# Local attention as banded matmuls in chunks that run into the next layer's prologue, and one softmax check at the end in place of flags and branches

## The chip, the cores and the metric

The kernel runs on one core of one Trainium2 chip. The metric is device time in microseconds (us). The engines are PE (TensorE), DVE (VectorE), ACT (ScalarE), POOL (GpSimd) and SP (SyncE, which here issues DMAs).

## The reference

Four layers work on 2048 tokens of width 512, each with a layer norm and a residual. Layers 1 and 3 ("A") are local attention: 32 heads of 16, and each token looks at itself and the seven tokens at distances 2, 4, ... 14 before it. Layers 2 and 4 ("B") are full attention with 32 query heads and one shared key/value head. Shortened:

```python
def _A_ref(x, wqkv, wo):                       # H = 32, Dh = 16, W, dil = 8, 2
    q, k, v = ...                              # (x @ wqkv) split in heads
    idx = pos[:, None] - (jnp.arange(W) * dil)[None, :]
    logits = einsum("bhsd,bhswd->bhsw", q, k[idx]) * Dh ** -0.5   # -1e9 where idx < 0
    o = einsum("bhsw,bhswd->bhsd", softmax(logits), v[idx])
    return merge(o) @ wo
def _B_ref(x, wq, wk, wv, wo):                 # one k and v of width 16 for all heads
    p = softmax(einsum("bhqd,bkd->bhqk", q, k) * Dh ** -0.5)
    return merge(einsum("bhqk,bkd->bhqd", p, v)) @ wo
x = A_x
x = x + _A_ref(layernorm(x), A_wqkv, A_wo);  x = x + _B_ref(layernorm(x), B_wq, B_wk, B_wv, B_wo)
# ... and both once more, with the same weights
```

## The kernel before

Layer A puts 4 chunks of 512 tokens on 4 partition groups and computes each of the 8 window positions as elementwise products on DVE, which PE sums over the head dimension through an identity matrix. Its steps follow each other over the whole sequence.

```python
def layer_A_ch(...):
    ...
    last = layernorm_T(...)                    # all 16 token tiles: norm, transpose
    for d in range(DH):
        proj(0, d)                             # q: 16 matmuls of 512 columns and one ACT copy
        proj(1, d)                             # k
    if NCH > 1:
        nc.sync.dma_start(out=K[32:PCH, :, 0:PAD], in_=K[0:PCH - 32, :, 512:KW])
    for w in range(W):
        lg = ps1.tile([PCH, 512], F32, name="lg", tag="ps1")
        for hf in range(2):
            nc.vector.tensor_tensor(out=prod[:], in0=Q[:, dsl, :],
                                    in1=K[:, dsl, PAD - DIL * w:PAD - DIL * w + 512], op=ALU.mult)
            for d in range(DP):
                nc.tensor.matmul(lg[:], lhsT=ident[:PCH, :PCH], rhs=prod[:, d, :], ...)
        ...                                    # scale, mask the first tokens, running maximum
    ...                                        # v projection, subtract, exp, sum, reciprocal, multiply
    ...                                        # attn * v on DVE, summed on PE; output projection; residual
    if fill_end:
        pe_filler(nc, scratch[:], ident[:], wo_r4[:, 0, :], fill_end)
```

Layer B has a prologue (norm, q/k/v, and a bound on the norms of q and k) which writes a flag. The flag is loaded to a register and picks a fast or a slow attention, so there is a branch around each B:

```python
def layer_B(...):
    prologue_B(tc, x_sb, wq_sb, ..., flag_slot, ...)
    ...
    if mode == "fast":
        fast()
    ...
    else:                                      # mode "auto", as the kernel runs
        cond = nc.values_load(flag_slot, min_val=0, max_val=1)
        with tc.If(cond > 0) as cmp:
            fast()
        with cmp.Else():
            slow()
```

The end of the fast B is a serial chain: copy the last output block out of PSUM, send the softmax sums through DRAM to spread them over partitions, multiply (on POOL), project, add.

```python
def normalize(b, X, S2):
    chain("dve", nc.vector.reciprocal(out=S2[:], in_=S2[:]))
    ...                                        # DMA S2 -> rd (DRAM), DMA rd -> lb (broadcast)
    nc.gpsimd.tensor_tensor(out=onc[qc][:, t, :], in0=X[:], in1=lb[:], op=ALU.mult)
...
for qi in range(4):                            # after the last step
    emit_y(NQC - 1, qi, (opp, dvp)[qi % 2], ("o_ps", "dv")[qi % 2])   # 4 matmuls with woB, then the add
    run_later(10 ** 9)
```

## Time and profile before

The median is 1880.2 us (three runs, 1879.33 to 1886.67; a fourth, counted in the result below, makes it 1880.72); the profiled execution took 1883.3 us. The first view below is of the kernel before, cut into its four stages: A plus B's prologue, B's attention, and both again. The columns are the stretch, its length, then busy time and instruction count of each engine, granted clock, DMA share and GB/s.

```profile
core 0: us, PE busy (x) PEld busy (x) DVE busy (x) ACT busy (x) POOL busy (x), PEclk, DMA share, GB/s
0.00:227.00 227.00, 171.61 (x1598) 96.45 (x1610) 156.88 (x240) 80.05 (x121) 18.96 (x48) 0.97 0.12 32
227.00:945.00 718.00, 591.90 (x5683) 190.38 (x5688) 682.78 (x1116) 690.72 (x512) 23.36 (x16) 0.98 0.05 11
945.00:1162.00 217.00, 173.14 (x1599) 98.78 (x1610) 145.01 (x213) 75.64 (x116) 14.97 (x24) 0.91 0.01 2
1162.00:1880.00 718.00, 569.90 (x5682) 196.46 (x5688) 675.58 (x1088) 689.70 (x512) 23.50 (x16) 0.98 0.06 14
```

B is full: ACT is busy 690 of 718 us. The two A stages, 227 and 217 us, are not: PE is busy 76 and 80%, DVE 69 and 67%. The change is aimed at those.

The second view is the timeline of the kernel before where the first B ends and the third layer starts (columns: start, busy time, engine and line, operation, output from inputs, shape, count, and in brackets the idle time before and what ended it):

```profile
914.60 8.37 ACT L522 ACTIVATE pt<-st 128x1536 bf16<-128x1536 f32 x6
...
932.80 3.60 SPq L587 DMA_DIRECT2D lb<-rd  x8
938.18 1.26 POOL L591 TENSOR_TENSOR onc<-X,lb 128x512 bf16<-128x512 f32 x1 [37.37 <-DMA lb<-rd]
939.50 0.61 PE L598 MATMUL o_ps<-woB_sb,onc 128*128 128x512 bf16 x1 [12.92 <-POOL onc L591]
...
945.21 0.69 DVE L609 TENSOR_TENSOR x_sb<-x_sb,dv 128x512 f32<-128x512 f32 x1 [0.23 <-PE dv L598]
...
949.78 0.38 DVE L91 TENSOR_SCALAR ln_ve<-mv_next 128x4 f32<-128x4 f32 x4 [2.94 <-issue]
951.48 0.81 ACT L99 ACTIVATE xn<-x_sb,ln_nmr,ln_rstd 128x512 bf16<-128x512 f32 x1 [28.51 <-DVE ln_nmr L93]
953.94 4.91 PE L109 MATMUL pT<-ident,xn 128*128 128x128 bf16 x36 [8.77 <-DVE xn L103]
```

The last attention exponential (`pt`) ends at 914.60 + 8.37 = 922.97. The DMA chain for the last sums ends at 938 (PE waits 12.9 us for it), the last residual add at 945.9, and only then does the next layer start; its first transposes (`pT`) run at 953.94, 31.0 us after the last exponential. I use these marks for all kernels: first and last `pt` of each B, first transposes, first projection. The stretch from B1's last exponential to B2's first is called the gap; here it is 239.2 us.

### The profile page before, as it was taken

How to read it: one execution, taken by the hardware profiler on the slowest of the kernel's cores; microseconds unless marked ns; L12 is line 12 of the kernel's file. 1: busy time of each engine (PE TensorE's matmuls, PEld its weight loads, DVE VectorE, ACT ScalarE, POOL GpSimd, SP SyncE). 2: the span in 40 equal slices, each digit the busy share in tenths (PEclk: the TensorE clock that was granted, in tenths of full speed). 3: DMA queues.
4: the chain of work that ended last, by engine and by line, in shares of the span. 5: the costliest groups of instructions: out<-in, count | busy, mean ns of one | idle time of the engine just before them, and what ended most of it. 6: DMA issues, size and time to landing. Idle time of an engine off the chain costs nothing.

```text
span 1883.3 us, 35972 instructions
## 1 busy us (share of the span) xinstructions
PE 1506.5 (80%) x14548; PEld 582.1 (31%) x14596; DVE 1660.3 (88%) x2657; ACT 1536.1 (82%) x1261; POOL 80.8 (4%) x104
## 2 busy tenths in 40 slices
PE   5888787878888887898677887777788788877884
PEld 4443322222222222222163443222222222222221
DVE  4797599999999999999628976999999999999995
ACT  5231599999999999999652326999999999999994
POOL 2001000000000000000010010000000000000000
PEclk9999899999999999999879988999999999999998
DMA  3020000000000000000000000000000000000000
GB/s 102 2 47 1 1 4 12 16 10 10 10 11 10 10 10 10 11 13 11 16 3 2 2 1 1 10 10 10 10 10 21 10 10 10 22 13 13 25 11 22
DMA packets 48403, 25.23 MB, mean 13 GB/s; under 512 B 36320, under 2 KB 41440, under 8 KB 48096
## 3 DMA queue, kind: packets, MB, share of 16 engines
q1 hardware_dynamic: 48224, 22.80, 5.4%
q8 instruction: 118, 1.93, 0.4%
q14 instruction: 61, 0.50, 0.1%
HBM read 15.24 MB, written 2.62 MB: 9 GB/s over the span
## 4 chain that ended last, share of the span: by engine, by line
DVE 36%; ACT 28%; PE 19%; issue 12%; SPq 2%; DMA 2%; POOL 1%; DVEq 0%; POOLq 0%; ACTq 0%
ACT pt L522 27%; DVE tt L528 12%; DVE it L533 12%; PE o_ps L541 4%; PE st L516 3%; PE ps L194 3%; DVE prod L219 2%; PE dv L516 2%; PE y L275 2%; PE ps L364 2%; SPq L571 1%; DVE X L564 1%; DVE pv L263 1%; PE acc L266 1%; DVE ln_stats L89 1%
## 5 line engine op out<-in xcount | busy, mean ns | idle before, releaser
L522 ACT ACTIVATE pt<-st 128x1536 bf16<-128x1536 f32 x1024 | 1380.4, 1742 | 21.1 <-PE dv L516 19.4
L528 DVE TENSOR_SCALAR tt<-dv 128x512 int16<-128x512 f32 x1024 | 701.6, 685 | 46.3 <-PE dv L516 12.5
L533 DVE TENSOR_SCALAR it<-tt 128x2048 int16<-128x2048 int16 x1024 | 711.6, 696 | 0.0
L516 PE MATMUL st<-QT,KAB 32*128 32x512 bf16 x3072 | 406.5, 386 | 201.3 <-ACT pt L522 183.6
L541 PE MATMUL o_ps<-it,VE 128*32 128x512 bf16 x4096 | 440.3, 387 | 17.3 <-DVE it L533 15.9
L541 PE MATMUL o_ps<-pt,VE 128*32 128x512 bf16 x3072 | 411.0, 392 | 5.9 <-DVE X L564 2.3
L516 PE MATMUL dv<-QT,KAB 32*128 32x512 bf16 x1024 | 390.8, 382 | 19.7 <-DVE tt L528 15.4
L541 PEld LDWEIGHTS <-VE 128*32 128x32 bf16 x7168 | 212.1, 93 | 530.8 <-issue 496.1
L516 PEld LDWEIGHTS <-KAB 32*128 32x128 bf16 x4096 | 161.9, 91 | 469.8 <-issue 454.7
L219 DVE TENSOR_TENSOR prod<-Qch,Kch 128x4096 bf16<-128x4096 bf16 x32 | 72.4, 2279 | 58.0 <-ACT Kch L198 56.6
L99 ACT ACTIVATE xn<-x_sb,ln_nmr,ln_rstd 128x512 bf16<-128x512 f32 x44 | 33.8, 807 | 102.9 <-DVE ln_nmr L93 92.9
L591 POOL TENSOR_TENSOR onc<-X,lb 128x512 bf16<-128x512 f32 x32 | 46.9, 1464 | 1379.2 <-DMA lb<-rd 1009.4
L194 PE MATMUL ps<-xnT,w_sb 128*32 128x512 bf16 x1536 | 90.6, 391 | 1.9 <-ACT Vch L198 1.8
L194 PEld LDWEIGHTS <-w_sb 128*32 128x32 bf16 x1536 | 79.9, 141 | 12.1 <-issue 7.5
L266 PE MATMUL acc<-pv,ident 128*128 128x512 bf16 x250 | 67.6, 400 | 16.7 <-DVE pv L263 11.0
L222 PE MATMUL lg<-prod,ident 128*128 128x512 bf16 x250 | 60.3, 380 | 19.1 <-DVE prod L219 18.8
L263 DVE TENSOR_TENSOR pv<-attn,Vch 128x2048 bf16<-128x2048 bf16 x64 | 73.2, 1218 | 1.2 <-PE acc L266 1.2
L268 ACT CAST Och<-acc 128x2048 bf16<-128x2048 f32 x8 | 14.9, 1865 | 71.9 <-PE acc L266 71.9
L224 ACT ACTIVATE L<-lg 128x512 f32<-128x512 f32 x16 | 9.6, 597 | 70.8 <-PE lg L222 70.8
L109 PE MATMUL pT<-ident,xn 128*128 128x128 bf16 x256 | 29.1, 270 | 38.3 <-ACT xn L99 26.6
L598 PE MATMUL o_ps<-woB_sb,onc 128*128 128x512 bf16 x86 | 29.8, 407 | 32.9 <-POOL onc L591 26.0
L266 PEld LDWEIGHTS <-ident 128*128 128x128 bf16 x256 | 25.4, 101 | 58.8 <-issue 24.4
(157 smaller groups left out, 607.2 us busy)
## 6 DMA issues: line engine op xcount, KB each, us to landing
lb<-rd SPq DMA_DIRECT2D x256, 32.0 KB, 1.8
xi<-in_A_x_dram SPq DMA_DIRECT2D x4, 512.0 KB, 5.5
wo_r_73<-in_A_wo_dram SPq DMA_DIRECT2D x4, 512.0 KB, 7.5
out_dram<-xo SPq DMA_DIRECT2D x4, 512.0 KB, 3.7
w_sb<-in_A_wqkv_dram SPq DMA_DIRECT2D x4, 384.0 KB, 7.9
wq_sb<-in_B_wq_dram SPq DMA_DIRECT2D x4, 128.0 KB, 2.1
woB_sb<-in_B_wo_dram SPq DMA_DIRECT2D x4, 128.0 KB, 2.6
X<-X_3114 SPq DMA_DIRECT2D x4, 32.0 KB, 2.6
```

The lines of the kernel that those rows point to most:

```text
L194: nc.tensor.matmul(ps[32 * c:32 * c + 32, :], lhsT=wqkvP[:, kt, j, d, :], rhs=xnT[:, kt, c * 512:(c + 1) * 512], start=(kt == 0), stop=(kt ...
L219: nc.vector.tensor_tensor(out=prod[:], in0=Q[:, dsl, :], in1=K[:, dsl, PAD - DIL * w:PAD - DIL * w + 512], op=ALU.mult)
L222: nc.tensor.matmul(lg[:], lhsT=ident[:PCH, :PCH], rhs=prod[:, d, :], start=(hf == 0 and d == 0), stop=(hf == 1 and d == DP - 1))
L263: nc.vector.tensor_tensor(out=pv[:], in0=attn[:, w, :].unsqueeze(1).to_broadcast([PCH, DG, 512]), in1=V[:, ds_, PAD - DIL * w:PAD - DIL * ...
L266: nc.tensor.matmul(acc[:, i, :], lhsT=ident[:PCH, :PCH], rhs=pv[:, i, :], start=(w == 0), stop=(w == W - 1))
L275: nc.tensor.matmul(ys[c][:], lhsT=O[32 * c:32 * c + 32, d, i * 128:(i + 1) * 128], rhs=wo_r4[32 * c:32 * c + 32, d, :], start=(d == 0), st ...
L516: chain("pe", nc.tensor.matmul(out, lhsT=KAB[32 * g:32 * g + 32, a, kt * 128:(kt + 1) * 128], rhs=QT[32 * g:32 * g + 32, t, qc * 512:(qc + ...
L522: nc.scalar.activation(out=pt[:], in_=st_tiles.pop(s)[:], func=AF.Exp, scale=scale)
L528: chain("dve", nc.vector.tensor_scalar(out=t_tiles[m][:, r, :], in0=dv_tiles.pop(s)[:], scalar1=T_SCALE, scalar2=T_BIAS, op0=ALU.mult, op1 ...
L533: chain("dve", nc.vector.tensor_scalar(out=it[:].bitcast(I16), in0=t_tiles[m][:], scalar1=0.25, scalar2=127.0 * 128.0 + J_OFF[j], op0=ALU. ...
L541: chain("pe", nc.tensor.matmul(o_ps[b][32 * g:32 * g + 32, :], lhsT=VE[:, kt, j, :], rhs=rhs, start=(b, g) not in started, stop=stop, tile ...
L591: nc.gpsimd.tensor_tensor(out=onc[qc][:, t, :], in0=X[:], in1=lb[:], op=ALU.mult)
```

## The change

The intent is to take A off DVE and to let the phases overlap.

- Tokens are stored even first, then odd, so the dilated window becomes a band of 8 neighbours. Scores of 64 keys against 72 queries are one small matmul. The band mask is added on PE by a matmul with the identity; one exponential without maximum follows.
- Values and sums are small matmuls into PSUM; dividing is exp(-log(sum)) on ACT and one multiply.
- A is chunked (4 chunks of 512 tokens), and each chunk's B prologue follows its A output at once. A with the B prologue is called a phase below; there are two.
- The norm flags and the branches around B go. POOL gathers squared logarithms and sums; one test at the end leads to a slow program if they are out of bounds.

```diff
+class Phase:
+    def __init__(...):
+        self.sps = pool("As", 2, space=PSUM)
+        self.ops = pool("Ao", 1, space=PSUM)
+        self.mps = pool("Am", 2, space=PSUM)
+        ...
+        vp = pool("Av", 1)
+        self.vbuf = [vp.tile([128, 8, 4, 2, 2, 32], BF16, name=f"V{i}") for i in range(3)]
+        self.nhalf = vp.tile([128, 4], F32, name="nhalf")
+        nc.gpsimd.memset(self.nhalf[:], -0.5)
+        for v in self.vbuf:
+            nc.vector.memset(v[:], 0.0)
...
+    def a_attn(self, c):            # per unit: masks, scores, exp, values, sums
+                    for j in range(2):
+                        nc.tensor.matmul(st[:, j, 0:ncol], lhsT=self.w.ident[:], rhs=self.w.band[:, 0:ncol],
+                                         start=True, stop=False)
...
+                            nc.tensor.matmul(st[:, j, col:col + w], lhsT=kk[gs, t, kb, :, :],
+                                             rhs=q[gs, t, q0:q0 + w], start=False, ...)
...
+            nc.scalar.activation(out=logs[:], in_=dn[:], func=AF.Ln)
+            nc.scalar.activation(out=rec[:], in_=logs[:], func=AF.Exp, scale=-1.0)
+            nc.vector.tensor_tensor(out=onc[:, t, :], in0=o[:], in1=rec[:], op=ALU.mult)
+            self.checks.see_logs(logs[:], tmp[:])           # two POOL operations
...
+    def run(self, plan0):
+        self.a_in(0, plan0)
+        self.a_in(1, plan)
+        for c in range(4):
+            self.a_attn(c)
+            if c + 2 < 4:
+                self.a_in(c + 2, plan)
+            self.a_out(c)
+            self.b_in(c, plan)
...
-        cond = nc.values_load(flag_slot, min_val=0, max_val=1)
-        with tc.If(cond > 0) as cmp:
-            fast()
-        with cmp.Else():
-            slow()
...
+    for pair in range(nlayers // 2):
+        ...
+            with ExitStack() as c2:
+                ph = Phase(c2, tc, x_sb, x_bf if pair == 0 else None, w, QT, KAB, VE, checks, f"p{pair}")
+                ph.run(("a", "v", "a", "v"))
+            with ExitStack() as c2:
+                attn_B_fast(c2, tc, QT, KAB, VE, w.woB, x_sb, S, f"b{pair}", checks, ov if last else None)
+    ...
+        bad = checks.flag(cps)
+    cond = nc.values_load(bad[0:1, 0:1], min_val=0, max_val=1)
+    with tc.If(cond > 0):
+        slow_net(...)
```

The norm statistics that B took for the next layer, and the matmuls that filled PE's time at A's end, also go; the input is loaded as bfloat16 without a cast.

## The prediction

> **What bounds the kernel now.** (Busy times by window, and the timeline.) The span of 1883 us has two attention-B stages of 718 us (227 to 945, 1162 to 1880), ACT busy 690 us in each and DVE 676 to 683. B runs at ACT's pace: back-to-back exponentials take 1.33 us each, and PE idles 0.40 us per step waiting for the `pt` exponential to free its PSUM. The rest, 227 + 217 = 444 us, is local attention (A) plus the B prologue, twice. There no engine is full: projections are PE-bound (32 us), q·k products DVE-bound (34), softmax (17), a·v products DVE-bound (45), output projection PE-bound (18), prologue (49: PE 37, DVE 32). The phases follow each other, so different engines' limits add up.
>
> **What the change does.** Only those 444 us change. The B loop keeps its instructions (16 statistics, 13.6 us of DVE, leave the first B; the second, without them, also takes 718 us, so I expect nothing from that).
> Removed: DVE products (73 us per A layer), identity-matrix sums, max/subtract/reciprocal passes, K/V halo copies, norm checks, flags and branches around B.
> Added per phase (A plus prologue): 64 units, each of 2 mask matmuls, 8 to 10 score, 16 to 20 value and 4 to 6 denominator matmuls.
>
> Estimates per phase, from durations in the trace:
> - DVE about 90 us, ACT 100, POOL 95 (squared logs at 1.3 to 1.5 us each, key masks at 0.77).
> - PE: projections, transposes and outputs about 84 us (0.217 us per full 512-column matmul). A unit about 1.7 us: masks 0.25; 26 small weight-load/matmul pairs at 27 to 40 ns (16 such pairs took 0.55 us in the prologue; the Trainium skill, "TensorE: Matmul & The Clock Gate", section Back-to-back issue gap, gives a floor of about 25 ns); denominators 0.3; four changes of tile shape at 0.1 us. The skill's "TensorEngine Tiling (Array Packing)", Key Properties, says that a change of tiling mode drains the array; the trace agrees: value matmuls start about 0.1 us after the scores have streamed. So 64 units cost about 110 us and PE about 195 us.
>
> So the phase becomes PE-bound, and the gain is overlap, not less PE work: about 195 us of PE plus start and the serial last output/prologue (10 to 15) = 205 to 215 us for the first, against 227. In the second, B's tail (18 us from last exponential to last output) can overlap with chunks 0 and 1, since no branch separates them: about 190 against 217. Flag waits before B (3 us each) go; the final check and branch cost about 5.
> Sum: about 40 us gained. I shade it to 55, as small pairs may run nearer the floor.
>
> **Predicted: 1825 us, 80% range 1750 to 1890.** Faster by over 2%: 0.62; within 2%: 0.30; slower: 0.08.
>
> **What would show it.** Both B stages within 1% of 718 us. In the A phases PE busiest (over 85%), ACT, DVE and POOL below 60%, phases of 180 to 215 us. Small pairs start 27 to 40 ns apart. Phase 2 matmuls start before B's last output add.
>
> **What would make it wrong.** Small pairs at 60 ns or more (a unit then takes 2.4 us, and the change loses); the single-buffered output and denominator banks leaving PE idle for the logarithm-exponential-multiply chain (2 us, 16 times per phase) without fill; POOL's masks and checks holding up scores; the next prologue not interleaved; or much faster pairs and fewer drains (phases of 160 us, about 1765 total).

## The result, and the profile after

The kernel after takes 1856.36 us (median of four runs, 1855.17 to 1859.7) against 1880.72. The ratio is 0.9867, interval 0.9842 to 0.9892. That is 24 us, or 1.3%, where 55 were predicted. The outputs are right in all runs of this document.

The profiled execution was 1853.3 us, 30 us under the profiled one before, so the profiles overstate the difference by some 6 us. Its stages:

```profile
0.00:209.00 209.00, 173.32 (x2751) 99.51 (x2771) 88.96 (x192) 97.03 (x172) 114.24 (x151) 0.94 0.09 27
209.00:926.00 717.00, 575.60 (x5690) 193.71 (x5698) 683.43 (x1112) 689.87 (x515) 34.71 (x69) 0.98 0.05 11
926.00:1130.00 204.00, 173.00 (x2747) 98.53 (x2767) 82.47 (x170) 95.87 (x172) 106.19 (x87) 0.90 0.01 2
1130.00:1850.00 720.00, 571.20 (x5681) 194.86 (x5694) 678.20 (x1095) 690.41 (x515) 30.77 (x48) 0.98 0.06 14
```

B is unchanged, as it should be. In the phases PE is busy as long as before (173 us), DVE a little over half as long, POOL six to seven times as long. PE is now 83 and 85% busy. The hand-over from the first B, in the timeline of the kernel after:

```profile
896.63 6.11 ACT L817 ACTIVATE pt<-st 128x1536 bf16<-128x1536 f32 x4
...
902.80 0.40 PE L682 MATMUL s<-bandmask,ident 128*128 128x288 bf16 x2 [1.54 <-ACT pt L817]
...
905.84 0.69 DVE L596 BATCH_NORM_STATS2 stats<-x_sb 128x6 f32<-128x512 f32 x1 [1.56 <-PE o_ps L836]
...
914.21 3.63 SPq L510 DMA_DIRECT2D lb<-rd  x8
919.39 1.26 POOL L512 TENSOR_TENSOR onc<-X,lb 128x512 bf16<-128x512 f32 x1 [7.60 <-DMA lb<-rd]
920.72 0.61 PE L868 MATMUL o_ps<-woB_sb,onc 128*128 128x512 bf16 x1 [12.73 <-POOL onc L512]
...
925.86 0.69 DVE L879 TENSOR_TENSOR x_sb<-x_sb,dv 128x512 f32<-128x512 f32 x1 [0.41 <-PE dv L868]
925.95 0.10 POOL L573 MEMSET nhalf<- 128x4 f32 x1 [5.29 <-PE dv L868]
926.13 2.00 POOL L599 TENSOR_TENSOR rstd<-ve,nhalf 128x4 f32<-128x4 f32 x2
926.93 1.76 DVE L575 MEMSET V_14061<- 128x2048 uint32 x1 [0.38 <-issue]
929.07 1.76 DVE L575 MEMSET V_14062<- 128x2048 uint32 x1 [0.38 <-issue]
931.21 1.76 DVE L575 MEMSET V_14063<- 128x2048 uint32 x1 [0.38 <-issue]
932.89 0.17 DVE L600 SCALAR_TENSOR_TENSOR nmr<-mv,rstd 128x4 f32<-128x4 f32 x2
...
933.96 2.29 PE L614 MATMUL pT<-ident,xn 128*128 128x128 bf16 x16 [8.13 <-ACT xn L606]
...
937.08 8.21 PE L621 MATMUL ps<-xnT,w_sb 128*128 128x512 bf16 x24 [0.82 <-DVE xnT L586]
```

The last `pt` ends at 902.75 (896.63 + 6.11, rounded), the first transposes run at 933.96: 31.2 us later, the same as before. There is no branch any more, and still nothing of the next layer's PE work has moved ahead except four band masks (`s`, from 902.80), which need no input of the layer. PE waits 12.7 us for the sums' DMA chain with nothing else to do. The norm's inputs were early: statistics of the first three chunks ran from 905.84. What holds the norm is `nhalf`, a constant of 4 columns. Its memset waits for B's last output matmul (5.29 us, "PE dv L868"), which I read as memory that B used before, and DVE's three memsets of fresh value buffers stand ahead of `nmr` in DVE's queue.

The same marks for the kernels that matter below (times in us from the span's start; the last three columns are counted from B1's last exponential or are the gap):

| kernel | first projection | B1's first `pt` | first transposes of phase 2 | its first projection | gap |
|---|---|---|---|---|---|
| before | 30.8 | 227.3 | +31.0 | +41.2 | 239.2 |
| after | 16.7 | 209.3 | +31.2 | +34.3 | 227.3 |
| before_nobranch | 30.8 | 225.5 | +6.7 | +28.9 | 223.3 |
| all2 | 16.9 | 210.5 | +10.1 | +13.9 | 222.0 |
| all2_tail | 16.7 | 208.2 | +11.4 | +15.2 | 215.7 |
| all2_dve | 16.8 | 210.7 | +10.1 | +13.9 | 211.5 |

The 30 us between the profiles are then: phase 1 -18, gap -12, both B's and the tail about 0. From first projection to first `pt` the kernel before took 196.5 and 198.0 us, the kernel after 192.5 and 193.0. So most of the first phase's gain is an earlier start: projections begin after 4 transposed tiles in place of 16, and the other 12 hide behind PE's work.

The marks also tell how far the medians can be trusted. The gap repeats where the hand-over is the same: 227.3 us in the kernel after, 227.2 in after_copy and 227.5 in noif. The rest repeats less well. With the same code, after_copy has B1's first `pt` at 212.2 us, 2.9 us later; and the two B stages, each from its first `pt` to its last, take 1390.2 us together in after_copy and 1382.8 in `both`, whose edit leaves B's code alone. The granted clock differs from run to run, too: in all2 the run of 1841.05 us has a mean of 0.970, that of 1851.81 us 0.963. So what an edit does to the hand-over is read from the gap below, and the difference of the medians overstates it: about 12 us against 4.2 for `both`, 9 against 5.3 for all2, 21.7 against 15.8 for all2_dve.

### The profile page after: what moved, and what is told of

Same layout as the page of the kernel before. It is cut to its first block, busy times and chain, and to the rows that moved or that the text cites. A ratio compares the mean times of both kernels' runs of the same rounds, so it can differ in the third digit from the quotient of the medians.

```text
span 1853.3 us, 41000 instructions
## 1 busy us (share of the span) xinstructions
PE 1493.1 (81%) x16864; PEld 586.6 (32%) x16929; DVE 1533.1 (83%) x2568; ACT 1573.2 (85%) x1371; POOL 285.9 (15%) x354
## 5 line engine op out<-in xcount | busy, mean ns | idle before, releaser
L836 PE MATMUL o_ps<-it,VE 128*32 128x512 bf16 x4096 | 442.0, 387 | 16.9 <-DVE it L828 15.9
L692 ACT ACTIVATE P<-s 128x576 bf16<-128x576 f32 (+1 forms) x128 | 78.9, 650 | 50.4 <-PE s L688 50.2
L718 DVE TENSOR_TENSOR onc<-o,rec 128x512 bf16<-128x512 f32 x32 | 22.1, 691 | 98.7 <-ACT rec L717 98.7
L638 POOL TENSOR_SCALAR k<-kt,kmask 128x512 bf16<-128x512 bf16 x64 | 99.0, 1566 | 6.0 <-ACT kt L585 6.0
L682 PE MATMUL s<-bandmask,ident 128*128 128x288 bf16 (+1 forms) x256 | 58.5, 297 | 7.4 <-POOL bandmask L532 5.8
L621 PE MATMUL ps<-xnT,w_sb 128*128 128x512 bf16 x244 | 62.1, 400 | 2.5 <-DVE xnT L586 0.8
L606 ACT ACTIVATE xn<-x_sb,nmr,rstd 128x512 bf16<-128x512 f32 x13 | 10.5, 812 | 52.7 <-DVE nmr L600 52.7
L586 DVE CAST q<-ps 128x512 bf16<-128x512 f32 x32 | 22.1, 691 | 40.0 <-PE ps L621 35.7
L614 PE MATMUL pT<-ident,xn 128*128 128x128 bf16 x256 | 27.4, 249 | 34.2 <-POOL xn L610 17.8
L585 ACT CAST kt<-ps 128x512 bf16<-128x512 f32 x32 | 18.7, 585 | 40.4 <-PE ps L621 40.4
L868 PE MATMUL o_ps<-woB_sb,onc 128*128 128x512 bf16 x87 | 29.9, 407 | 28.2 <-POOL onc L512 12.7
L711 PE MATMUL dn<-P,halves 128*64 128x256 bf16 (+3 forms) x576 | 44.7, 232 | 9.5 <-ACT P L692 9.5
L446 POOL TENSOR_TENSOR tmp<-logs 128x512 f32<-128x512 f32 x32 | 33.3, 1040 | 114.2 <-ACT logs L716 114.2
```

The lines of the kernel that those rows point to most:

```text
L446: self.nc.gpsimd.tensor_tensor(out=tmp, in0=logs, in1=logs, op=ALU.mult)
L621: self.nc.tensor.matmul(ps[:], lhsT=wcols(kt), rhs=xnT[:, kt, :], start=(kt == 0), stop=(kt == 3))
L638: nc.gpsimd.tensor_scalar(out=k[:, t, :, a, :], in0=kt_[:].rearrange("p (b i) -> p b i", i=64), scalar1=self.w.kmask[:, a:a + 1], scalar2= ...
L682: nc.tensor.matmul(st[:, j, 0:ncol], lhsT=self.w.ident[:], rhs=self.w.band[:, 0:ncol], start=True, stop=False)
L692: nc.scalar.activation(out=P[:, :, 0:ncol], in_=st[:, :, 0:ncol], func=AF.Exp, scale=DH ** -0.5)
L711: nc.tensor.matmul(out, lhsT=self.w.halves[:, gh, :], rhs=rhs, start=first("d", j), stop=False, skip_group_check=True, tile_position=(0, 6 ...
```

## The experiments

Twelve kernels ran, three calls of four. Each was timed beside the kernel before. The kernel after ran again as after_copy; it is compared with kernels of other calls through the ratios to the kernel before, and by medians where the difference is large.

| run | median, us | ratio to before | 95% interval |
|---|---|---|---|
| after_copy | 1857.74 | 0.9871 | 0.9851 to 0.9892 |
| both | 1845.99 | 0.9814 | 0.9788 to 0.9840 |
| tail_only | 1852.56 | 0.9852 | 0.9830 to 0.9874 |
| tail_over | 1849.18 | 0.9824 | 0.9800 to 0.9849 |
| all2 | 1848.40 | 0.9830 | 0.9804 to 0.9857 |
| all2_tail | 1838.07 | 0.9786 | 0.9763 to 0.9808 |
| noif | 1855.02 | 0.9873 | 0.9850 to 0.9896 |
| nologs | 1856.30 | 0.9887 | 0.9865 to 0.9909 |
| mask2 | 1881.30 | 1.0004 | 0.9988 to 1.0020 |
| before_nobranch | 1865.44 | 0.9915 | 0.9897 to 0.9933 |
| hoist | 1849.11 | 0.9823 | 0.9805 to 0.9841 |
| all2_dve | 1836.09 | 0.9775 | 0.9756 to 0.9794 |

### First call: memory of the second phase, and the order on PE

**after_copy**: the kernel after, unchanged.

> The changed kernel unaltered, as the base for the other runs of this call. Both theories: 1855 to 1860 us, ratio to the kernel before 0.986 to 0.989; 227 us between the last exponential of the first B stage and the first exponential of the second.

Measured 1857.74, as the first time.

**both**: the constant is made once, the value buffers are opened first in the phase, and the PSUM pools change places, so that the phase waits for other memory of B.

```diff
+        vp = pool("Av", 1)                      # now ahead of the phase's other pools
+        self.vbuf = [...]; self.nhalf = w.nhalf # nhalf made once, at the kernel's start
         self.sm = pool("Asm", 2)
...
-        self.ops = pool("Ao", 1, space=PSUM)
         self.mps = pool("Am", 2, space=PSUM)
+        self.ops = pool("Ao", 1, space=PSUM)
```

> The second local phase gets its memory early: value buffers first in SBUF, the -0.5 constant kept from the start, the PSUM banks of its projections on those that B's scores free first. PE's program order still has the last B output projection ahead of the first projections. Theory M (late memory and the clearing of the value buffers hold the second phase back): the gap of 227 us shrinks by 15 or more. Theory O (PE's fixed program order, written by the scheduler, holds it back, and memory only adds the clearing): it shrinks by 6 to 8, the time of the three clearings, total about 1849. Theory P (the phase is bound by PE throughput, the tail does not matter): under 3.

Measured 1845.99, about 12 us under after_copy. The first transposes moved from +31.2 to +19.7 us, but the projections still began only behind the 16 output matmuls, at +29 us. The three memsets now ran among B's last DVE work, where they delay the statistics; they were moved, not removed. The gap is 223.1 us, only 4.2 under that of after_copy; what made the B stages of this run shorter as well is not known.

**tail_only**: B1's last output projections come after the first chunk's projections in PE's order (their input is kept in a buffer of its own); nothing else.

```diff
     def run(self, plan0, tail=None):
         self.a_in(0, plan0)
+        if tail is not None:
+            self.b_tail(tail)                   # the 16 matmuls with woB and 4 adds
         self.a_in(1, plan)
```

> Only the order: the last output projection of the first B stage is written into the program after the projections of chunk 0 of the next phase (its input kept in a buffer of its own); memory as in the changed kernel. Theory M: under 3 us, since the constant and the value buffers still wait for B's normalisation. Theory O: 5 to 12, limited by the clearing that ends near 927. Theory P: under 3.

Measured 1852.56, 5 us under after_copy; the intervals overlap. The gap did not shrink, it is 228.1 us: the projections began at +28.6 in place of +34.3, but from there to B2's first `pt` it took 199.5 us in place of 193.0. By itself the deferral brought nothing at the hand-over.

**tail_over**: both edits together.

> Order and memory together. Theories M and O together: the gap of 227 us shrinks by 17 to 22, total 1836 to 1841 us, 0.976 to 0.979 of before; first transposes of the second phase within 10 us of B's last exponential instead of 31. Theory P: under 5 us, total above 1850.

Measured 1849.18: no better than `both` alone. The projections began 6 us sooner after the last exponential, but from there to B2's first `pt`, where the deferred matmuls now lie, it took 199.6 us against 194.1, and the gap is 222.1 against 223.1. In the three edits the gap changed by -4, +1 and -5 us. None of the theories named that; nearest is P, by which the tail doesn't matter, and all2_dve below speaks against it. The gain expected from a full overlap, 17 to 22 us, came in no run of this call. What all four had in common were the memsets in DVE's queue at the hand-over.

### Second call: no memsets at the hand-over; the check; POOL's load

**all2**: value buffers and constant are allocated and zeroed once for both phases. To make room, the bfloat16 input is released after the first phase, and B's Q/K/V store is shared by the pairs; the PSUM order is that of `both`.

```diff
-        vp = pool("Av", 1)
-        self.vbuf = [...]; self.nhalf = ...; memsets
+        self.vbuf, self.nhalf = w.vbuf, w.nhalf
...
             if pair == 0:
-                pass
+                xpool.close()                   # the bfloat16 input
+            else:
+                vpool.close()                   # the value buffers, ahead of the last B
```

> Edit: the kernel after, with the value buffers and the -1/2 constant allocated once for both phases (their zeroing runs once, at the start), the Q/K/V store of B shared, the bfloat16 input released after the first phase, and the PSUM pools of the phase in the order scores, misc, outputs. Theory Z (the zeroing of fresh buffers stands ahead of the second phase's statistics on VectorE): first transposes of phase 2 by 912 us (31 us after the last B1 exponential in the kernel after, now about 10), gap from the last B1 exponential to the first B2 exponential 214 to 219 us (after: 227), total about 1838 to 1842. Theory D (the start of phase 2 is set by the last normalisation's DMA chain and the 16 output-projection matmuls that stand first in PE's order, not by the zeroing): transposes earlier, but projections still at about 931; gap 221 to 224, as in the run 'both', total 1845 to 1848.

Measured 1848.40, gap 222.0. The transposes came 21 us sooner (+10.1 in place of +31.2), as theory Z has it, and even the projections did (+13.9 in place of +34.3), which theory D had denied. Yet the gap shrank by 5 us only: D's number for the gap came out, and its total within half a microsecond, for a reason that D hadn't named. The timeline of all2 shows where the 20 us went:

```profile
915.11 3.62 SPq L510 DMA_DIRECT2D lb<-rd  x8
...
921.79 9.27 POOL L633 TENSOR_SCALAR k<-kt,kmask 128x512 bf16<-128x512 bf16 x6 [0.25 <-ACT kt L580]
...
927.18 0.41 PE L643 MATMUL pv<-w_sb,xnT 128*64 128x256 bf16 x4
...
931.02 1.27 POOL L512 TENSOR_TENSOR onc<-X,lb 128x512 bf16<-128x512 f32 x1
...
932.35 0.61 PE L863 MATMUL o_ps<-woB_sb,onc 128*128 128x512 bf16 x1 [4.76 <-POOL onc L512]
```

The DMAs that bring `lb` were issued by 918.7; in the kernel after, POOL's multiply started 1.6 us after the issues ended (914.21 + 3.63 to 919.39). Here it ran at 931.02: six key masks of the next layer's first chunk, 1.55 us each, stood ahead of it in POOL's queue. PE then waited 4.76 us for it. The Trainium skill, "PSUM — Partial Sum Buffer", section Engine vs sequencer instructions, says "ScalarE/VectorE/GpSimdE queues are strict FIFO"; the trace agrees, with 11 us between the time at which the data should have been there and the multiply.

**all2_tail**: as all2, with B1's last output projections after the first chunk's projections.

> Edit: as all2, and B1's last four output projections issued after the first chunk's projections of phase 2. Theory D: PE can start the projections by about 917 to 920, gap 213 to 218, total 1837 to 1842, some 5 to 8 us below all2. Theory Z: same as all2 within 2 us (the zeroing was the whole wait). Theory P (PE throughput, phase 2 is a fixed amount of PE work after the point where PE starts): gap falls only by PE idle time recovered, about 5 us below all2, not by the 4 us of deferred matmuls.

Measured 1838.07, 10 us under all2, of which the gap, 215.7, shows 6; theory Z (the same as all2) falls, and theory D's gap and total came out. The multiply still ran late (929.11), but PE had the value projections to do meanwhile. The deferral that brought nothing on top of `both` pays once the projections can start.

**noif**: the kernel after without the final test's branch and the slow program.

> Edit: the kernel after without the final check's branch: the flag is computed but not read, and there is no rescue program (result right for these inputs). The prediction put the final check and branch at +5 us. If right: 1851 to 1853. Rival (the check is hidden behind the last normalisation and the last output's DMA, as the tail of 28.3 us against 27.9 before suggests): 1856 to 1858, same as the kernel after within 1.5 us.

Measured 1855.02, ratio 0.9873 against 0.9871: the final branch costs nothing that these runs resolve, and the prediction's 5 us are not there. In the trace of the kernel after, the test's flag is ready 6 us before the last DMA chain lets POOL multiply, so it is hidden.

**nologs**: the kernel after without the POOL operations on the logarithms.

> Edit: the kernel after without the squares of the logarithms on GpSimd (2 operations of 1.0 and 1.3 us, 16 times per phase: 37 us of GpSimd's 114 per phase). Result right for these inputs. Theory P (a phase is limited by PE and its chain, GpSimd has slack): phases shorter by at most 2 us each, total 1853 to 1858. Rival G (GpSimd holds key masks and normalisations back): phases 5 to 15 us shorter each, total 1828 to 1847.

Measured 1856.30, no faster (0.9887). POOL's total fell from 114 to 77 us in the first phase, and the phases stayed: 209.0 and a gap of 225.6. POOL's amount of work doesn't limit the phases; its order at the hand-over is another matter.

### Third call: PE's load, the branches alone, POOL's order

**mask2**: each band mask is added twice (the result stays right).

```diff
                     for j in range(2):
-                        nc.tensor.matmul(st[:, j, 0:ncol], ..., start=True, stop=False)
+                        for rep in range(2):
+                            nc.tensor.matmul(st[:, j, 0:ncol], ..., start=(rep == 0), stop=False)
```

> Edit: the kernel after with each of the two band-mask matmuls per unit issued twice (the second adds the same mask again; where it is zero nothing changes, elsewhere -30000 becomes -60000, so the result stays right). It adds 128 matmuls of 288 columns per phase; a pair of masks takes about 0.24 to 0.36 us of PE in the trace, so 64 units add 15 to 23 us of PE time per phase. Theory P (PE time is what a phase costs, other engines have slack): each phase 14 to 23 us longer, total 1885 to 1903. Theory L (a phase is set by the chains exponential, logarithm, multiply, and PE's 15% idle time absorbs additions): each phase under 8 us longer, total under 1873.

Measured 1881.30, 23.6 us over after_copy; the phases grew by 12.7 and 11.5 us. The timelines show what was added, first of the kernel after (start to next start 0.35 us for a pair of masks; the last two lines show 16 value matmuls in 0.23 us, which is used further below), then of mask2 (0.60 us for four):

```profile
100.69 0.42 PE L682 MATMUL s<-bandmask,ident 128*128 128x288 bf16 x2
101.04 0.30 PE L688 MATMUL s<-q,k 32*128 32x72 bf16 x8
...
102.66 0.31 PE L697 MATMUL o<-P,V_236 64*32 64x72 bf16 x16
102.89 0.32 PE L711 MATMUL dn<-P,halves 128*64 128x256 bf16 x4
```

```profile
100.95 0.67 PE L683 MATMUL s<-bandmask,ident 128*128 128x288 bf16 x4
101.55 0.30 PE L689 MATMUL s<-q,k 32*128 32x72 bf16 x8
```

That is 0.25 us for each of 64 units, 16 us per phase. About three quarters of it lengthened the phase (roughly: against after_copy's own trace the first phase grew by about 10 us only). This is under the 14 us that theory P asked for, and above theory L's 8: a phase is mostly, not wholly, paced by PE. One rival stays: the added masks also stand ahead of each unit's own scores and exponential, so this run doesn't tell PE's amount of work from a chain of steps that passes through PE.

**before_nobranch**: the kernel before with its `mode` set to "fast". The norms are still bounded and flags written, but nothing loads them, and only the fast B is built.

```diff
-    mode: str = "auto",
+    mode: str = "fast",
```

> Edit: the kernel before in its mode without the norm flags' loads and the branches around B (only the fast B is built, the rest unchanged). The prediction booked 6 us for the flag waits of both layers, beside the 40 us summed from the phases. If they are a separate gain: 1872 to 1876. Rival (they lie within the A stages' ends or the compiler-ordered start, so little is won): 1878 to 1882. If removing the branches lets the second layer overlap B's tail as the prediction has it: below 1865.

Measured 1865.44, ratio 0.9915: 15.5 us from one word, more than half of what the whole change brings. Phase 1 lost 1.8 us (which holds the flag's wait, but is no more than first phases of the same code differ), the gap 15.9. The timeline of before_nobranch:

```profile
912.96 7.43 ACT L522 ACTIVATE pt<-st 128x1536 bf16<-128x1536 f32 x5
...
927.08 0.86 PE L109 MATMUL pT<-ident,xn 128*128 128x128 bf16 x12 [3.10 <-DVE xn L103]
...
937.36 1.26 POOL L591 TENSOR_TENSOR onc<-X,lb 128x512 bf16<-128x512 f32 x1 [7.38 <-DMA lb<-rd]
...
949.33 16.02 PE L194 MATMUL ps<-xnT,w_sb 128*32 128x512 bf16 x270
```

The transposes of the 12 finished tiles run from 927.08, 6.7 us after the last exponential (912.96 + 7.43), in the 14 us in which the DMA chain runs. The old layer A memsets fresh memory ahead of its norm too, but on POOL, in 0.3 us each, and the first one runs at 922.50, once the last attention matmuls are done and not the output projection. So the gap of this kernel, 223.3 us, is 4 us shorter than that of the kernel after.

**hoist**: `both` without the change of PSUM order.

> Edit: as the run 'both' but with the PSUM pools in the order of the kernel after: only the -1/2 constant is made once and the value buffers are allocated first in each phase. It splits 'both' (-11.7 us against the kernel after). If the buffers' place did it all: 1844 to 1848, first transposes of phase 2 about 19 us after the last B1 exponential. If the PSUM order did it: 1855 to 1859.

Measured 1849.11 (0.9823), by the intervals the same as `both` (0.9814): the PSUM order did nothing that shows. The first transposes here ran at 931.79, 27.4 us after the last exponential (904.40), later than the 19 us expected; yet the gain is that of `both`; the projections, which PE does next, began at +29.9 and +29.0 us. (One `pt` of hoist runs early, inside the phase, so its gap isn't comparable; from B1's last `pt` to B2's last it took 914.5 us, `both` 914.2 and the kernel after 922.2.) An early first transpose alone isn't the gain.

**all2_dve**: as all2, and the last normalisation's multiply of each B on DVE.

```diff
-        nc.gpsimd.tensor_tensor(out=out, in0=X[:], in1=lb[:], op=ALU.mult)
+        (eng or nc.gpsimd).tensor_tensor(out=out, in0=X[:], in1=lb[:], op=ALU.mult)
...
+        eng = nc.vector if qc == NQC - 1 and t == 3 else None
```

> Edit: as all2, and the last normalisation multiply of each B on VectorE instead of GpSimd. In all2's trace this multiply stood behind six key-mask operations in GpSimd's queue (ran at 931.0 us though its data had landed by about 920) and PE waited 4.8 us for it. Theory Q (GpSimd's in-order queue cost all2 its gain): multiply at about 927, PE's wait before the output projection under 1 us, gap 217 to 218.5 against 222, total 1842 to 1845. Rival (the wait only moves, to the first attention's chain): gap 221 to 223, total as all2, 1846 to 1850.

Measured 1836.09, ratio 0.9775 (0.9756 to 0.9794): 12 us under all2 and 21.7 under after_copy by the medians, and over 2% faster than the kernel before with the interval clear of 0.98. The gap is 211.5, 10.4 under all2 and 6 less than theory Q expected. Its timeline:

```profile
911.08 2.29 PE L609 MATMUL pT<-ident,xn 128*128 128x128 bf16 x16 [4.82 <-ACT xn L601]
...
912.50 3.61 SPq L510 DMA_DIRECT2D lb<-rd  x8
...
914.90 9.69 PE L616 MATMUL ps<-xnT,w_sb 128*128 128x512 bf16 x32 [1.52 <-ACT xnT L580]
...
924.37 0.68 DVE L512 TENSOR_TENSOR onc<-X,lb 128x512 bf16<-128x512 f32 x1
...
925.10 0.39 PE L864 MATMUL o_ps<-woB_sb,onc 128*128 128x512 bf16 x1
925.33 1.03 PE L864 MATMUL dv<-woB_sb,onc 128*128 128x512 bf16 x4
926.27 1.02 PE L864 MATMUL o_ps<-woB_sb,onc 128*128 128x512 bf16 x4
927.13 1.02 PE L864 MATMUL dv<-woB_sb,onc 128*128 128x512 bf16 x4
```

PE has no wait left ahead of the output projection. There is a second gain: four such matmuls now take 0.86 us from start to start (926.27 to 927.13), while in the kernel after, behind 12.7 us of idle PE, and in all2, behind 4.76 us, they took 1.7 us. The granted clock in these stretches is 0.50 in all2 and 1.00 here. The Trainium skill, "TensorE: Matmul & The Clock Gate", section Back-to-back issue gap, gives for a single matmul of N columns N/1.2 ns cold (at the low clock) and N/2.4 + 2.5 ns warm, so 427 and 216 ns for 512 columns; the trace agrees with both, 0.43 and 0.215 us each. (Its lower figure for a stream is taken up in the last section.)

## Why the prediction was wrong

It said 55 us and 24 were measured. Point by point:

- **Both B stages unchanged: right.** 717 and 720 us in the table of windows against 718.
- **Phase 1 in 205 to 215 us against 227: right in sum by luck, as two misses cancel.** It took 209. PE's work was overestimated: 173 us busy, not about 195. Small pairs were cheaper than priced: 16 value pairs take 0.23 us (102.66 to 102.89 in the timeline shown beside mask2), about 15 ns each with the change of tile shape behind them, where I took 27 to 40. The 0.55 us for 16 pairs from which I took this is the length of a timeline row, up to the modelled end of the last matmul; in the trace those pairs start 25 ns apart. But PE idles some 36 us, where I took 10 to 15 for the start and the end together. The phase is PE-paced to about three quarters (mask2), not wholly.
- **"In the second, B's tail ... can overlap with chunks 0 and 1, since no branch separates them: about 190 against 217": the step that failed.** I expected -27 us there, with B's tail of 18 us running beside the next layer; the gap fell by 12, and none of that is overlap of the tail: about 7 is the earlier first projection (+34.3 against +41.2), 5 the stretch after it. Taking the branch away does permit the overlap: it is worth 15.5 us on its own in the kernel before. But the kernel after put a wait of its own in the same place: fresh buffers, of which the memset of `nhalf` waits for B's last matmul and those of the value buffers stand ahead of the norm in DVE's queue, so phase 2's first transposes stayed at +31 us. When the zeroing is done once (all2) the start moves by 20 us, and POOL's queue, with the next layer's key masks ahead of B's last multiply, takes most of it back. With both away (all2_dve) the gap is 211.5, 15.8 us under that of the kernel after and 27.7 under that of the kernel before. So the overlap had about the predicted size; the kernel's allocation and queue order kept it from happening. The two causes were tried together with shared storage and an early release of the input; what those bring by themselves was not tried.
- **"Flag waits before B (3 us each) go": counted twice.** They lie inside the 227 and 217 us that the phase estimates were already set against. Phase 1 of before_nobranch is shorter by 1.8 us, within what first phases of the same code differ.
- **"The final check and branch cost about 5": wrong, nothing that shows.** noif is within 0.3% and its ratio is the same; the test hides behind a DMA chain.
- **"I shade it to 55, as small pairs may run nearer the floor": wrong.** The pairs did run faster, but this gain was spent on PE idle that I had not counted, and the phase didn't shorten with it.

By size, roughly: the prediction's terms sum to 40 to 50 us (12 to 22 for phase 1, 27 for phase 2, 6 for the flags, less 5 for the check), and the shading makes it 55. The profiles show 30. Of the 25 us between, about 15 are the overlap that didn't happen, 6 the flags, 5 the other way the check, and the rest, about 9, the shading. The medians show another 6 us less than the profiles.

A rival that POOL's amount of work holds the phases back (nologs) fell. That the PSUM order matters fell too (hoist against `both`). How PE's idle time in a phase (36 us in the first) divides among the chains stays open. That chunking's early start is most of phase 1's gain is read from the marks, not tried.

## What to carry to other kernels

Taking a branch away only permits overlap; whether it comes depends on what stands first in each engine's queue, so look at the hand-over for memsets of fresh buffers and for next-stage work ahead of the last stage's closing operation. Allocate and zero once what two stages share, and put the closing operation of a serial DMA chain on an engine whose queue has nothing long ahead of it. Read what an edit does from the stretch that it touches, as the total also moves with the clock and with stages that were not edited. When a change bundles two ideas, price each alone: here one word in the old kernel gave over half the gain.

## What the Trainium skill lacked or had wrong

- "TensorE: Matmul & The Clock Gate", section Back-to-back issue gap, has an issue floor of about 25 ns for up to 64 columns. For pairs on separate 64-row, 32-column tiles of the array these traces show 16 matmuls of 72 columns, with their weight loads, in 0.23 us, about 15 ns each to the next group's start; a floor per tile would fit, but no run here isolates it. The section also has about 131 ns per matmul of 512 columns in a stream of weight loads and matmuls; such streams take 215 ns each here (all2_dve, 926.27 to 927.13 for four).
- "GPSIMD Engine Reference", section 3.1, has a time for a two-input add and the cost of a tight loop over 512 elements, 769 ns, which matches the plain one-input normalisation on POOL here (774 ns, bfloat16). The key mask, of the same size with a rearranged output, took 1566 ns: twice that. The page's section 7 prices reads with large strides, but nothing that I found prices a rearranged output; that the output is the cause was not tested.
- "TensorEngine Tiling (Array Packing)", section Key Properties, says that a change of mode drains the array but gives no time; the traces here have about 0.1 us between a mask pair's streaming (0.24 us for the two further masks of mask2) and the next start (0.35 us for the pair).
- No page that I found says what a memset of reused memory waits for at a stage's border. Here a 0.10 us memset of 4 columns waited 5.29 us for B's last matmul, and the norm of the next layer with it.
